# Moving the squares, the start of group 0 and two scalings in a fused attention and MLP kernel

## The chip, the cores and the metric

One core of one Trainium2 chip. The metric is device time in microseconds (us), the median of several executions; the six of the kernel before lie between 433.15 and 436.11 us. Each run also has a mean granted clock of TensorE over the span (1.0 is full speed); a stretch below it is called cold here, one at 1.0 warm. In the profiles PE is TensorE and PEld its weight loads, ACT is ScalarE, DVE is VectorE, Pool is GpSimd, and SPq is the queue on which SyncE issues transfers.

## The reference

For 8 batches and 12 heads, q and k (448 tokens of 64 numbers) are normed and weighted, softmax attention follows, and its output goes through a two-layer MLP:

```python
q_n, k_n = rmsnorm(q, g_q), rmsnorm(k, g_k)        # x / sqrt(mean(x*x) + 1e-6) * g
attn = softmax(q_n @ k_n.T / 8)
x = (attn @ v)  ->  (3584, 768)
h = x @ w_in                                        # 768 x 2048
g = max(h, 0) + alpha * min(h, 0)
out = g @ w_out                                     # 2048 x 768
```

## The kernel before

The 24 groups (`y`, three a batch, each of two pairs of heads) flow through all engines. For each group and each of q and k: a load into `nat`; squares on ACT or Pool; sums on DVE; two small ACT functions make the reciprocal root `rr`; a scaling to fp16 `qs` on DVE or Pool; transposes (on TensorE for the first six groups, by transposing transfers after that) into `qT` and `kT`. Then scores on TensorE, an exponential on ACT for each of seven tiles a group, sums over keys (`dn`), products with v (`av`), and the MLP (`hT` and `op`). Scores come in "bursts" of mostly two tiles. Where an instruction waited, those behind it on its engine waited too: the 2.93 us below are a case.

```python
def square(y, nm):
    src = nat[y, nm].rearrange("p h j d -> p (h j d)")
    sq = ld.tile([128, 2 * J, D], FP32, name="sq", tag="sq", bufs=4)
    sqf = sq.rearrange("p n d -> p (n d)")
    if y < 2:
        nc.scalar.activation(out=sqf, in_=src, func=AF.Square)
    else:
        nc.gpsimd.tensor_mul(out=sqf, in0=src, in1=src)
    sqs[y, nm] = sq

def scale(y, nm):
    t = ld.tile([128, J, 2, D], FP16, name="qs", tag="qs", bufs=4)
    eng = nc.vector if (y, nm) in ((0, "k"), (1, "q"), (2, "q"), (3, "q")) else nc.gpsimd
    eng.tensor_mul(out=t..., in0=nat[y, nm], in1=rr_t[y]...)     # cut
    qs[y, nm] = t

# where squares and sums are called: at = ahead of burst n, after = behind it      (cut)
    at(n - (6 if early else 4 if y <= 3 * G else 5), load_qk, y)
    for nm in "qk":
        (after if early else at)(n - 2, square, y, nm)
        if early:
            after(n, reduce, y, nm)
        else:
            jobs.setdefault(n, []).append((reduce, (y, nm)))
    roots[n + 1] = y

# the start                                                       (loads cut)
    spin(3)                     # filler matmuls
    spin(18, False)
    ...
    for nm in "qk":
        square(0, nm); reduce(0, nm)
    ...
    for nm in "qk":
        root(0, nm); scale(0, nm)
    ...
    square(1, "q"); turn(0); square(1, "k"); load_v(0); square(2, "q")
    for nm in "qk":
        reduce(1, nm)
    after(0, root, 1)
    for nm in "qk":
        after(0, scale, 1, nm)
    after(0, square, 2, "k")
    after(0, load_w_in, 0)
    ...
    roots[3] = 2                # root and both scalings of group 2 in burst 3
```

## Time and profile before

| | before |
|---|---|
| time, median | 433.94 us in the first 3 runs, 434.32 over 6 |
| span of the profiled run | 432.8 us |
| TensorE busy | 418.0 us, 97 % |
| ACT, DVE, Pool busy | 278.6, 204.3, 175.6 us |
| mean granted clock | 1.0 |
| chain that ended last | TensorE 81 %, ACT 5 %, DMA 5 %, DVE 4 %, Pool 2 % |

Busy shares over the whole span hide that the stages differ: one reads them by stretches of time. The lines for that are in the prediction. Bracketed at the end of a timeline line stands how long the engine was idle ahead of the instruction, and what ended that.

### The profile page before, as it was taken

Reading aid. Unit: us, or ns where it says so; the run is one execution under the profiler, and the core shown is the slowest. Engines: PE = TensorE matmul, PEld = TensorE weight load, DVE = VectorE, ACT = ScalarE, POOL = GpSimd, SP = SyncE. Lnnn points to the kernel's source line nnn. Section 1 sums busy time; section 2 is a strip of 40 time slices with the busy share of each in tenths; the row PEclk is TensorE's granted clock in tenths of the full one; section 3 lists DMA queues with packets and bytes.
Section 4 is the critical chain, followed back from the end, with each engine's and each line's share of the span. In section 5 each row is a group of like instructions: output and inputs, shape, how many; then the busy total and the mean of one; then the engine's idle time right before and its main releaser. Section 6 shows DMA issues by size and latency. Waiting matters only on the chain.

```text
span 432.8 us, 11487 instructions
## 1 busy us (share of the span) xinstructions
PE 418.0 (97%) x4965; PEld 216.8 (50%) x4965; DVE 204.3 (47%) x304; ACT 278.6 (64%) x385; POOL 175.6 (41%) x133
## 2 busy tenths in 40 slices
PE   8789899999999999999999999999999999999996
PEld 3344344444455445544555445554555445555554
DVE  3756564445545463546444463545453353233421
ACT  4898888668876677757667577757757577132300
POOL 5799693495464617083253626074133000000000
PEclk9999999999999999999999999999999999999999
DMA  8999899989787734967086743944082300211133
GB/s 192 236 235 215 146 211 190 206 151 200 171 120 179 180 82 67 201 109 186 20 157 142 164 118 63 202 99 113 20 153 52 77 1 21 56 38 31 25 73 75
DMA packets 70387, 53.85 MB, mean 124 GB/s; under 512 B 37424, under 2 KB 70336, under 8 KB 70336
## 3 DMA queue, kind: packets, MB, share of 16 engines
q1 hardware_dynamic: 55536, 40.19, 42.2%
q0 software_dynamic: 13984, 11.81, 18.1%
q10 hardware_dynamic: 816, 1.11, 1.0%
q8 instruction: 39, 0.64, 0.6%
q14 instruction: 12, 0.10, 0.1%
HBM read 45.62 MB, written 11.01 MB: 131 GB/s over the span
## 4 chain that ended last, share of the span: by engine, by line
PE 81%; ACT 5%; DMA 5%; DVE 4%; POOL 2%; issue 1%; DVEq 0%; POOLq 0%
PE op L365 26%; PE hT L327 20%; PE hTa L327 10%; PE sc L232 7%; PE opa L365 6%; PE dn L261 4%; PE av L261 4%; ACT expT L246 3%; DMA kT<-qs 3%; PE spin L394 2%; DMA nat<-in_k_dram 2%; PE avb L261 2%; DVE ss L154 2%; POOL qs L171 1%; DVE gT L355 1%
## 5 line engine op out<-in xcount | busy, mean ns | idle before, releaser
L246 ACT ACTIVATE expT<-sc,expb 128x896 f16<-128x896 f32 x168 | 161.4, 1003 | 36.5 <-PE sc L232 35.7
L365 PE MATMUL op<-w_out_sb,gT 128*128 128x384 f16 (+1 forms) x752 | 126.4, 323 | 0.0
L171 POOL TENSOR_TENSOR qs<-nat,rr 128x896 f16<-128x896 f32 x44 | 76.7, 1764 | 117.8 <-ACT rr L166 87.5
L365 PEld LDWEIGHTS <-gT 128*128 128x128 f16 x912 | 85.8, 98 | 65.4 <-issue 12.7
L327 PEld LDWEIGHTS <-w_in_sb 128*128 128x128 f16 x768 | 73.3, 98 | 75.1 <-issue 10.7
L327 PE MATMUL hT<-xT,w_in_sb 128*128 128x448 f16 x510 | 107.3, 353 | 1.9 <-DVE gT L355 1.1
L148 POOL TENSOR_TENSOR sq<-nat 128x896 f32<-128x896 f32 x44 | 73.4, 1681 | 40.5 <-DMA nat<-in_q_dram 36.6
L354 ACT ACTIVATE ah<-hT,cols 128x448 f16<-128x448 f32 x85 | 53.7, 633 | 44.2 <-PE hT L327 44.1
L355 DVE TENSOR_TENSOR gT<-hT,ah 128x448 f16<-128x448 f32 x85 | 52.8, 623 | 49.7 <-ACT ah L354 49.6
L377 DVE COPY osb<-op 128x384 f32<-128x384 f32 (+1 forms) x47 | 25.7, 548 | 86.8 <-PE op L365 86.8
L232 PE MATMUL sc<-qT,kT 64*32 64x448 f16 (+1 forms) x1092 | 53.6, 356 | 6.0 <-ACT expT L246 3.8
L154 DVE TENSOR_REDUCE ss<-sq 128x14 f32<-128x896 f32 x48 | 50.4, 1076 | 8.4 <-ACT sq L146 5.6
L327 PE MATMUL hTa<-xT,w_in_sb 128*128 128x448 f16 x246 | 53.2, 353 | 0.0
L354 ACT ACTIVATE ah<-hTa,cols 128x448 f16<-128x448 f32 x41 | 26.0, 633 | 31.4 <-PE hTa L327 31.4
L355 DVE TENSOR_TENSOR gT<-hTa,ah 128x448 f16<-128x448 f32 x41 | 25.5, 623 | 25.8 <-ACT ah L354 25.8
L232 PEld LDWEIGHTS <-kT 64*32 64x32 f16 (+1 forms) x1092 | 15.3, 93 | 38.6 <-issue 32.7
L365 PE MATMUL opa<-w_out_sb,gT 128*128 128x384 f16 x160 | 27.7, 327 | 0.6 <-DVE xT L312 0.6
L312 DVE TENSOR_TENSOR xT<-av,rden 128x896 f16<-128x896 f32 x16 | 17.4, 1090 | 17.6 <-PE av L261 14.2
L261 PEld LDWEIGHTS <-vt 64*32 64x32 f16 (+1 forms) x1260 | 18.9, 94 | 13.2 <-issue 2.2
L261 PE MATMUL dn<-expT,ones 64*32 64x448 f16 (+1 forms) x812 | 24.4, 350 | 1.1 <-issue 0.2
L261 PE MATMUL av<-expT,vt 64*32 64x448 f16 (+1 forms) x812 | 24.1, 350 | 0.0
L278 ACT ACTIVATE rden<-dn 128x896 f32<-128x896 f32 x16 | 14.5, 907 | 7.3 <-PE dn L261 7.3
(45 smaller groups left out, 162.0 us busy)
## 6 DMA issues: line engine op xcount, KB each, us to landing
out_dram<-osb SPq DMA_DIRECT2D x109, 96.0 KB, 2.3
nat<-in_q_dram SPq DMA_DIRECT2D x46, 224.0 KB, 5.3
nat<-in_k_dram SPq DMA_DIRECT2D x46, 224.0 KB, 5.5
vt<-in_v_dram POOLq DMA_DIRECT2D x16, 336.0 KB, 6.3
w_in_sb<-in_moe_w_in_dram POOLq DMA_DIRECT2D x12, 256.0 KB, 7.3
w_out_sb<-in_moe_w_out_dram POOLq DMA_DIRECT2D x4, 768.0 KB, 11.5
nat<-in_q_dram ACTq DMA_DIRECT2D x2, 224.0 KB, 4.5
nat<-in_k_dram ACTq DMA_DIRECT2D x2, 224.0 KB, 5.9
```

The lines of the kernel that those rows point to most:

```text
L148: nc.gpsimd.tensor_mul(out=sqf, in0=src, in1=src)
L154: nc.vector.tensor_reduce(out=ss_t[y][:, "qk".index(nm)].rearrange("p h j -> p (h j)").unsqueeze(2), in_=sqs[y, nm], axis=AXIS_X, op=ALU.add,)
L171: eng.tensor_mul(out=t.rearrange("p j h d -> p h j d"), in0=nat[y, nm], in1=rr_t[y][:, "qk".index(nm)].unsqueeze(3).broadcast_to((128, 2, ...
L232: nc.tensor.matmul(out=sc[ds(64 * g + m * c, m), par, :S].rearrange("p (j c) -> p j c", j=J), lhsT=kT[ds(64 * par, 64), j, g, ts(c, m)], r ...
L246: nc.scalar.activation(out=expT[y][:, j], in_=scs[y, j][:, :, :S], func=AF.Exp, scale=QK_SCALE, bias=expb[:, 0:1],)
L261: nc.tensor.matmul(out=accs[g][ds(m * h, m), :S], lhsT=weights(g, y, par, ts(c, m), j), rhs=expT[y][ds(64 * g, 64), j, par, :], start=(j = ...
L312: nc.vector.tensor_mul(out=x, in0=av[:, :, :S], in1=r)
L327: nc.tensor.matmul(out=hT[:, :S], lhsT=w_in_sb[:, g * G + i, ts(ft, 128)], rhs=xT[b][:, g, i, :], start=(i == 0 and g == 0), stop=(i == G ...
L354: nc.scalar.activation(out=ah, in_=hT[:, :S], func=AF.Copy, scale=alpha_sb[:, ft : ft + 1])
L355: nc.vector.tensor_max(out=gT[:, ft, ds((b & 1) * S, S)], in0=hT[:, :S], in1=ah)
L365: nc.tensor.matmul(out=ops[c][:, :PW], lhsT=gT[:, ft, ts(t, 128)], rhs=w_out_sb[:, ft, ds(oh * OH + c * PW, PW)], start=(ft == 0), stop=(f ...
L377: nc.vector.tensor_copy(out=o[:, ts(c, PW)], in_=ops[c][:, :PW])
```

## The change

It has three parts. The **start**: group 0 is squared and summed in pieces so that scores begin sooner; k of group 1 is squared on Pool; roots of groups 1 and 2 move inside a burst (`mid`), their scalings to the end of it. The **lead burst** (the one in which the first batch's attention ends and its MLP begins): two sums move behind the first MLP products. The **steady part**: from group 5 on, squares are called behind a burst, and so behind its scalings on Pool.

```diff
-        if y < 2:
+        if (y, nm) == (1, "q"):
             nc.scalar.activation(out=sqf, in_=src, func=AF.Square)
         else:
             nc.gpsimd.tensor_mul(out=sqf, in0=src, in1=src)
...
+    def part_square(nm, h, j, eng): ...       # and part_reduce, part_root, part_scale, part_turn, part_copy
...
         for nm in "qk":
-            (after if early else at)(n - 2, square, y, nm)
+            after(n - 2, square, y, nm)
...
-    spin(3)
-    spin(18, False)
+    spin(2)
+    spin(17, False)
...
+    for h in range(2):
+        part_square("q", slice(h, h + 1), full, nc.scalar)
+    for h in range(2):
+        part_reduce("q", slice(h, h + 1), full)
+    part_root("q", full)
+    part_scale("q", full, J, nc.gpsimd)
+    part_square("k", both, lo, nc.scalar)     # tokens 0 to 2 of 7
+    part_square("k", both, hi, nc.scalar)
...
-    after(0, root, 1)
-    for nm in "qk":
-        after(0, scale, 1, nm)
-    after(0, square, 2, "k")
-    after(0, load_w_in, 0)
+    mid[1] = 1
+    for nm in "qk":
+        after(1, scale, 1, nm)
+    after(1, square, 2, "k")
+    after(1, load_w_in, 0)
...
-    roots[3] = 2
+    mid[4] = 2
+    for nm in 'qk':
+        after(4, scale, 2, nm)
...
+            if n in mid and t == tiles[-1]:
+                root(mid[n])
             soft(*t)
...
-        if ups_first and n in dens:
+        if ups_first and n in dens and not lead:
...
-                if n in jobs:
+                if n in jobs and not (lead and done < 4):
...
         if not gaps[n] and n in turns:
+            if n < den_at[0]:
+                spin(1)
             turn(turns[n])
```

One consequence does not stand in the diff. Group 3's squares are called behind burst 4 too, by the loop that comes first; so in the built program they stand on Pool **ahead** of group 2's scaling of k.

More of the change, by code (lines that the diff above doesn't have):

```diff
@@ L169, in scale @@
         t = ld.tile([128, J, 2, D], FP16, name="qs", tag="qs", bufs=4)
-        eng = nc.vector if (y, nm) in ((0, "k"), (1, "q"), (2, "q"), (3, "q")) else nc.gpsimd
+        eng = nc.vector if nm == "q" and 0 < y <= G else nc.gpsimd
         eng.tensor_mul(
@@ L176, in scale, with part_square, part_reduce @@
         qs[y, nm] = t
+    tops = {}
+    def part_square(nm, h, j, eng):
+        if ("sq", nm) not in tops:
+            tops["sq", nm] = ld.tile([128, 2 * J, D], FP32, name="sq", tag="sq", bufs=4)
+        o = tops["sq", nm].rearrange("p (h j) d -> p h j d", h=2)[:, h, j]
+        src = nat[0, nm][:, h, j]
+        if eng is nc.scalar:
+            nc.scalar.activation(out=o, in_=src, func=AF.Square)
+        else:
+            eng.tensor_mul(out=o, in0=src, in1=src)
+    def part_reduce(nm, h, j):
+        if 0 not in ss_t:
+            ss_t[0] = ld.tile([128, 2, 2, J], FP32, name="ss", tag="ss", bufs=4)
+        nc.vector.tensor_reduce(
+            out=ss_t[0][:, "qk".index(nm), h, j].unsqueeze(3),
+            in_=tops["sq", nm].rearrange("p (h j) d -> p h j d", h=2)[:, h, j],
+            axis=AXIS_X, op=ALU.add,
+        )
@@ new lines, in part_root, with part_scale @@
+    def part_root(nm, j):
+        if 0 not in rr_t:
+            rr_t[0] = ld.tile([128, 2, 2, J], FP32, name="rr", tag="rr", bufs=4)
+        n = "qk".index(nm)
+        rr, ss = rr_t[0][:, n, :, j], ss_t[0][:, n, :, j]
+        nc.scalar.activation(out=rr, in_=ss, func=AF.Ln, scale=1.0 / D, bias=epsb[:, 0:1])
+        nc.scalar.activation(out=rr, in_=rr, func=AF.Exp, scale=-0.5)
+    def part_scale(nm, j, n, eng):
+        if (0, nm) not in qs:
+            qs[0, nm] = ld.tile([128, J, 2, D], FP16, name="qs", tag="qs", bufs=4)
+        eng.tensor_mul(
+            out=qs[0, nm][:, j].rearrange("p j h d -> p h j d"),
+            in0=nat[0, nm][:, :, j],
+            in1=rr_t[0][:, "qk".index(nm), :, j].unsqueeze(3).broadcast_to((128, 2, n, D)),
+        )
@@ new lines, in part_turn, with part_copy @@
+    def part_turn(nm, js):
+        if ("ps", nm) not in tops:
+            t = psf.tile([128, 512], FP32, name="tps", tag="mm")
+            tops["ps", nm] = t[:, :S].bitcast(FP16).rearrange("p (j c) -> p j c", j=J)
+        for j in js:
+            nc.tensor.transpose(
+                tops["ps", nm][:, j, :], qs[0, nm][:, j].rearrange("p h d -> p (h d)"), ident
+            )
+    def part_copy(nm, j, eng):
+        if (0, nm) not in qkT:
+            qkT[0, nm] = att.tile([128, J, 2, 64], FP16, name=f"{nm}T", tag=f"{nm}T", bufs=4)
+        o = qkT[0, nm].rearrange("p j g c -> p j (g c)")[:, j]
+        tp = tops["ps", nm][:, j]
+        if nm == "k":
+            nc.vector.tensor_scalar(
+                out=o, in0=tp, scalar1=gain[:, 0:1], scalar2=None, op0=ALU.mult
+            )
+        elif eng is nc.scalar:
+            nc.scalar.copy(out=o, in_=tp)
+        else:
+            eng.tensor_copy(out=o, in_=tp)
@@ L211, in turn @@
             o = t.rearrange("p j g c -> p j (g c)")
-            if nm == "q" and y == 0:
-                nc.scalar.copy(out=o, in_=tp)
-            elif nm == "q":
+            if nm == "q":
                 nc.vector.tensor_copy(out=o, in_=tp)
@@ L443 @@
     NB = len(bursts)
-    prep, post, roots = {}, {}, {}
+    prep, post, roots, mid = {}, {}, {}, {}
     def at(n, f, *a):
@@ L573 @@
     load_qk(2)
-    spin(3)
-    spin(18, False)
+    spin(2)
+    spin(17, False)
     ct = psf.tile([128, 512], FP32, name="ct", tag="mm")
     nc.tensor.transpose(ct[:, : NF + 2], rows, ident32[: NF + 2, : NF + 2])
-    spin(1)
-    for nm in "qk":
-        square(0, nm)
-        reduce(0, nm)
+    K0 = 3
+    both, full, lo, hi = slice(0, 2), slice(0, J), slice(0, K0), slice(K0, J)
+    for h in range(2):
[6 more added lines that the diff above has]
+    part_square("k", both, hi, nc.scalar)
+    part_reduce("k", both, lo)
+    part_reduce("k", both, hi)
+    part_root("k", lo)
+    part_scale("k", lo, K0, nc.vector)
+    part_root("k", hi)
+    square(1, "q")
     nc.vector.tensor_copy(out=cols, in_=ct[:, : NF + 2])
-    for nm in "qk":
-        root(0, nm)
-        scale(0, nm)
     nc.vector.tensor_mul(
@@ L589 @@
     )
-    square(1, "q")
-    turn(0)
+    part_turn("q", range(J))
+    part_turn("k", range(K0))
+    part_copy("q", full, nc.vector)
+    part_copy("k", lo, nc.vector)
+    load_v(0)
     square(1, "k")
-    load_v(0)
+    part_scale("k", hi, J - K0, nc.vector)
+    reduce(1, "q")
     square(2, "q")
+    after(0, part_turn, "k", range(K0, J))
+    after(0, part_copy, "k", hi, nc.vector)
+    after(0, reduce, 1, "k")
+    mid[1] = 1
     for nm in "qk":
-        reduce(1, nm)
-    after(0, root, 1)
-    for nm in "qk":
-        after(0, scale, 1, nm)
-    after(0, square, 2, "k")
-    after(0, load_w_in, 0)
+        after(1, scale, 1, nm)
+    after(1, square, 2, "k")
+    after(1, load_w_in, 0)
     for nm in "qk":
```

## The prediction

> **What bounds the kernel now.** I read four views: the page, the table by stretches of time, the waits of the matrix engine, and the timeline of the first 45 us. First the table by stretches (PE, PEld, DVE, ACT, POOL: busy us and instructions; then clock, DMA share, GB/s):
>
> ```profile
> 12.85:35.00 22.15, 19.02 (x305) 8.71 (x306) 14.97 (x18) 21.41 (x29) 20.69 (x15) 1.00 1.18 232
> 35.00:55.00 20.00, 17.96 (x163) 8.40 (x164) 11.38 (x17) 15.95 (x25) 16.15 (x15) 1.00 0.98 178
> 55.00:110.00 55.00, 52.28 (x545) 25.70 (x544) 28.38 (x42) 42.18 (x59) 35.13 (x25) 1.00 1.10 192
> 110.00:165.00 55.00, 54.85 (x671) 27.69 (x670) 27.55 (x41) 40.63 (x59) 24.81 (x16) 1.00 0.64 137
> ```
>
> From 110 us on TensorE is full (54.85 of 55.00 us), so nothing done to Pool, DVE or ACT there moves the end. From 12.85 to 35 us the full engines are ACT (21.41 of 22.15) and Pool (20.69); TensorE's 19.02 contain filler ("spin", 1.02 us each). So 12.85 to 35 us is bound by the stream of softmax exponentials on ACT and by Pool, which prepares q and k for it. A microsecond lost or won there moves everything behind it, since TensorE has no slack later to absorb it.
>
> The waits of TensorE over the whole span:
>
> ```profile
> PE sc L232 <- ACT expT L246: 3.8, 8, 1.0
> PE sc L232 <- DVE kT L217: 1.2, 2, 0.8
> PE hT L327 <- DVE gT L355: 1.1, 3, 0.5
> PE sc L232 <- DVE kT L192: 0.7, 2, 0.5
> ```
>
> Only "kT L192" (0.7 us) belongs to the steady part's q/k preparation: that is what any reordering of Pool after 56 us can win.
>
> The timeline (start, us, engine, line, instruction) where the change works:
>
> ```profile
> 8.68 1.69 POOL L171 TENSOR_TENSOR qs<-nat,rr 128x896 f16<-128x896 f32 x1 [4.37 <-ACT rr L166]
> ...
> 12.39 0.95 ACT L146 ACTIVATE sq<-nat 128x896 f32<-128x896 f32 x1
> ...
> 12.85 0.57 PE L232 MATMUL sc<-qT,kT 64*64 64x448 f16 x8 [0.78 <-DVE kT L217]
> ...
> 13.29 1.90 ACT L246 ACTIVATE expT<-sc,expb 128x896 f16<-128x896 f32 x2
> ...
> 15.69 1.09 DVE L171 TENSOR_TENSOR qs<-nat,rr 128x896 f16<-128x896 f32 x1 [0.90 <-ACT rr L166]
> 15.73 2.60 POOL L171 TENSOR_TENSOR qs<-nat,rr 128x896 f16<-128x896 f32 x1 [0.87 <-ACT rr L166]
> ...
> 19.91 1.48 POOL L124 DMA_DIRECT2D w_in_sb<-in_moe_w_in_dram  x2
> 21.38 0.73 POOL L127 DMA_DIRECT2D w_in_sb<-in_moe_w_in_dram  x1
> ...
> 22.36 2.58 POOL L171 TENSOR_TENSOR qs<-nat,rr 128x896 f16<-128x896 f32 x1 [0.24 <-ACT rr L166]
> 24.90 3.31 POOL L148 TENSOR_TENSOR sq<-nat 128x896 f32<-128x896 f32 x2
> ```
>
> The first exponential starts at 13.29 us. Pool scales group 2's k at 22.36, as soon as its root is there, and squares group 3 behind it. The same scaling takes 1.69 us alone and 2.6 us beside a DVE scaling.
>
> [...] 2.60 and 2.58 us for Pool's scaling beside DVE's 1.09, 1.69 beside a reduction. [...] an ACT root on 128x14 takes 0.21 us, a square on 128x896 0.95; my line is 0.2 us + 0.84 ns an element.
>
> **The change, part by part** (instruction orders of both built programs compared).
>
> 1. *Start of group 0.* q's square goes by heads, k's chain in token parts of 3 and 4; the copy of qT goes from ACT to DVE, and 1,k's square from ACT to Pool. Estimated pieces: square of 448 elements 0.57, 384: 0.52, 512: 0.63; reductions (1.08 for 896) 0.61, 0.54, 0.68; DVE scaling of the first k part 0.54. From q's landing at 5.31: squares end 6.40, second reduction 7.1, root 7.66; Pool scales q 7.75 to 9.44 (was 8.68 to 10.37). k landed at 7.20, but its squares now stand behind q's root: 7.63 to 8.73, reductions to 9.44, first part scaled 9.98. Then on DVE in order the copy of cols (0.18), gain (0.15), qT (0.62), first kT part (0.36): 11.27. Scores at about 11.3 instead of 12.85, first exponential about 11.8: **1.5 us earlier**.
>
> 2. *Group 1.* Its root now follows three exponentials instead of two, and waits for the second reduction, which on DVE stands behind k's second scaling, the first reduction (1.08), kT's second part (0.45): about 14.8, root ready 15.4 (was 15.65). Pool's scaling of k, 2.6 us beside DVE's, ends 18.1 (was 18.33). The transposes of group 1 thus come hardly earlier, and ACT, one tile ahead, idles for them. Of the 1.5 us some 0.2 are left.
>
> 3. *Group 2: the step that decides.* Before, Pool went: scaling of 1,k; square of 2,k; w_in issues; scaling of 2,k; two squares of group 3. The built program of the change has the two squares of group 3 **ahead** of the scaling of 2,k (it is called behind burst 4, after squares that stand there already). From 18.1: square 1.65, w_in issues 1.48 + 0.73, so 22.0; two squares 3.31, so 25.3; up to 0.9 for the collision with DVE's scaling of 2,q (2.6 less 1.69), so 26.2; scaling 1.69, so **27.8 instead of 24.94: 2.9 us later**. [...] the transposes of 2,k stand ahead of the scores of tile 12, so ACT runs dry although tiles of group 1 are left. Its exponential comes at 28.8 instead of 25.9.
>
> 4. *Lead burst.* Both reductions of group 5 (2.07 us at 41.67) move from ahead of the first gT products to between later ones. gT waits then only for ah (about 43.0 instead of 43.66): **0.5 us won**, the wait of hT on gT at 44.32.
>
> 5. *Steady part.* Squares go behind the scalings of a burst on Pool, same instructions. q and k reach their transposing DMAs some 3.3 us (two squares) earlier; worth at most the 0.7 us of kT L192: I take **0.6**.
>
> Sum: +2.9 − 0.5 − 0.6 = +1.8; a little less for what group 1's lead leaves (0.2): +1.6, so 435.5 us.
>
> **Rivals.** *A: the gain of the start survives*, because Pool reaches the squares of group 3 early enough to hide them. For it: Pool idles in the trace at 11.7 to 13.2. Against: until 22.0 Pool is laid out solidly, and the root of group 2 stands at 22.3. Then step 3 is gone, and 1.1 (one exponential and a bit) + 0.5 + 0.6 are won: about 431.7. *B: [...]* If 1,k's square starts on Pool before DVE's second k scaling (about 11.0 against 11.3), DVE waits 1.4 us, the root of group 1 slips by 1.2 and all of step 3 with it: about 436.7. Conversely, if DVE's scaling of 2,q is what waits, Pool saves 0.9: 434.6. *C: transfers bound the start.* DMA share is 0.87 before 12.85 us; the landing of 2,q (13.18) might slip with v's issue 0.9 us earlier. Then the square of 2,q, ending at 15.2, delays Pool by a few tenths. *D: the idle of TensorE cools it.* [...] step 3 leaves about 2.5. The trace has only 1.00 in the table above, so I give it little: up to +1.5 us.
>
> **Range and chances.** Step 3 may cost 2.0 to 4.0, steps 4 and 5 bring 0.3 to 1.5: 434.5 to 437.5. Rival A, to which I give one in six, pulls the lower end to 431.8; B and D together the upper to 438.2. Two per cent are 8.7 us, far more than any of these: faster 0.02, same 0.96, slower 0.02.
>
> **What would show it.** The first expT at about 11.8 (step 1); group 1's transposes within 0.4 us of 17.8 to 18.9 (step 2); Pool's second-group scaling ending about 27.8, behind two squares, and a gap of some 3 us in ACT's exponentials ahead of it (step 3); the first gT in the lead burst at once behind its ah (step 4); no wait for kT L192's successor (step 5), with TensorE as full from 110 us as before. The prediction is wrong if Pool's squares of group 3 end before group 2's root, or if the delay of 2.9 us is made up before 45 us by waits that I took for fixed.

## The result, and the profile after

The changed kernel took **438.56 us** (median of 6; 437.58 to 440.02), the kernel before 434.32. The ratio is 1.0097, with a 95 % interval of 1.0068 to 1.0126. A ratio here is the mean time of one kernel's fast runs over that of the other's in the same rounds, so not quite the ratio of the medians. The direction was foreseen; the size (+1.6 us over the first 433.94, range to 438.2) was not: the kernel lost about 4.2 us. The profiled run is the slowest of the six and one of the two coldest (440.02 us, clock 0.987), so what its profile shows of the clock is more than in a usual run (438.2 us, 0.996).

The same table by stretches, of the changed kernel (PE, PEld, DVE, ACT, POOL busy; then clock, DMA share, GB/s):

```profile
12.85:35.00 22.15, 16.65 (x162) 6.88 (x160) 14.45 (x13) 15.26 (x22) 15.52 (x14) 0.85 1.14 222
35.00:55.00 20.00, 18.85 (x282) 9.37 (x275) 12.90 (x17) 17.49 (x26) 16.98 (x14) 1.00 0.85 150
55.00:110.00 55.00, 51.70 (x540) 25.38 (x538) 28.08 (x41) 40.91 (x58) 39.01 (x28) 0.97 1.15 201
110.00:165.00 55.00, 54.85 (x607) 27.29 (x605) 27.91 (x44) 40.73 (x57) 21.32 (x14) 1.00 0.66 144
```

In the stretch that bounds the start, ACT works 15.26 us instead of 21.41; 4.77 us of the difference are one gap in the stream of exponentials, shown below. And the clock is 0.85. From 110 us on TensorE is as full as before (54.85 us). Three of TensorE's longest waits:

```profile
PE tps L268 <- DVE qs L171: 2.9, 1, 2.9
...
PE sc L292 <- DVE kT L254: 1.2, 1, 1.2
PE hT L387 <- DVE gT L415: 1.0, 1, 1.0
```

The first is new: group 2's transposes wait 2.9 us for a scaling on DVE, not on Pool. The timeline shows why. First the place in the kernel before, where the 13th exponential is the fifth of the eight at 22.17, so at about 25.9 us:

```profile
22.17 7.45 ACT L246 ACTIVATE expT<-sc,expb 128x896 f16<-128x896 f32 x8
...
22.30 1.09 DVE L171 TENSOR_TENSOR qs<-nat,rr 128x896 f16<-128x896 f32 x1 [0.64 <-ACT rr L166]
```

Then the changed kernel, where the 13th is the one at 29.75:

```profile
11.62 2.80 ACT L306 ACTIVATE expT<-sc,expb 128x896 f16<-128x896 f32 x3 [0.81 <-PE sc L292]
...
18.71 1.91 ACT L306 ACTIVATE expT<-sc,expb 128x896 f16<-128x896 f32 x2 [0.97 <-PE sc L292]
...
21.50 3.35 POOL L148 TENSOR_TENSOR sq<-nat 128x896 f32<-128x896 f32 x2
...
22.32 5.12 DVE L171 TENSOR_TENSOR qs<-nat,rr 128x896 f16<-128x896 f32 x1 [1.27 <-ACT rr L166]
...
24.79 1.71 POOL L171 TENSOR_TENSOR qs<-nat,rr 128x896 f16<-128x896 f32 x1
...
27.51 1.68 PE L268 MATMUL tps<-ident,qs 128*128 128x128 f16 x14 [2.93 <-DVE qs L171]
...
29.75 1.90 ACT L306 ACTIVATE expT<-sc,expb 128x896 f16<-128x896 f32 x2 [4.77 <-PE sc L292]
...
30.00 1.86 PE L454 MATMUL spin<-gT 128*128 128x448 f32 x2
```

Pool began two squares at 21.50 and went from them straight into the scaling of k. DVE's scaling of q, ready at 22.32, is recorded at 5.12 us, where it takes 1.09 elsewhere: it ended at 27.44, 0.94 us behind the last of Pool's three instructions (26.50). TensorE then had idled for 2.93 us, and the filler at 30.00 takes 1.86 us instead of the 1.02 of other places: the granted clock was 0.50 from 27.00 to 33.82 us. The packed traces have a record of the clock, from about 7 us on. In all 14 profiles a cold spell is at half clock and lasts 3.41 us or 6.83, save at the very end; here one of 6.83 begins at 27.00 us, 2.43 us into those 2.93 of idleness, and one of 3.41 at 85.02, after 1.24 and 0.62 us of idleness with four matmuls between (the 16 matmuls there took 4.44 us instead of 2.77), while the kernel before has none but at its end. A spell of 3.41 us takes 0.004 off the mean clock of a run (estimate: half of 3.41 over 438), so that 0.996, 0.992 and 0.988 go with one, two and three of them.

### The profile page after: what moved, and what is told of

Same layout as the page of the kernel before. It is cut to its first block, busy times and chain, and to the rows that moved or that the text cites.

```text
span 437.9 us, 11496 instructions
## 1 busy us (share of the span) xinstructions
PE 420.8 (96%) x4964; PEld 217.8 (50%) x4964; DVE 207.9 (47%) x309; ACT 278.0 (63%) x387; POOL 176.1 (40%) x134
## 4 chain that ended last, share of the span: by engine, by line
PE 80%; DMA 3%; DVE 2%; POOL 0%; issue 0%; ACT 0%
PE op L425 27%; PE hT L387 20%; PE hTa L387 10%; PE opa L425 7%; PE sc L292 6%; PE dn L321 4%; PE av L321 4%; DMA kT<-qs 3%; PE avb L321 2%; DVE osb L437 1%; DVE ss L154 0%; POOL sq L148 0%; DVE xT L372 0%; DVE gT L415 0%; PE tps L268 0%
## 5 line engine op out<-in xcount | busy, mean ns | idle before, releaser
L171 POOL TENSOR_TENSOR qs<-nat,rr 128x896 f16<-128x896 f32 x43 | 74.2, 1746 | 151.8 <-issue 101.3
L148 POOL TENSOR_TENSOR sq<-nat 128x896 f32<-128x896 f32 x45 | 74.6, 1680 | 7.7 <-DMA nat<-in_q_dram 5.0
L154 DVE TENSOR_REDUCE ss<-sq 128x14 f32<-128x896 f32 x46 | 48.4, 1076 | 0.8 <-POOL sq L148 0.7
L425 PE MATMUL opa<-w_out_sb,gT 128*128 128x384 f16 x160 | 29.4, 340 | 0.6 <-DVE xT L372 0.6
```

What stands on the lines that cost most here:

```text
L154: nc.vector.tensor_reduce(out=ss_t[y][:, "qk".index(nm)].rearrange("p h j -> p (h j)").unsqueeze(2), in_=sqs[y, nm], axis=AXIS_X, op=ALU.add,)
L171: eng.tensor_mul(out=t.rearrange("p j h d -> p h j d"), in0=nat[y, nm], in1=rr_t[y][:, "qk".index(nm)].unsqueeze(3).broadcast_to((128, 2, ...
L425: nc.tensor.matmul(out=ops[c][:, :PW], lhsT=gT[:, ft, ts(t, 128)], rhs=w_out_sb[:, ft, ds(oh * OH + c * PW, PW)], start=(ft == 0), stop=(f ...
```

## The experiments

The runs came in three sets, each on one chip and with its own runs of the kernel before (medians 434.6, 434.93 and 435.27 us). Every ratio below is to those; the 1.0097 above is to the runs of its own measurement. **Theory:** Pool's order ahead of group 2's scalings, with the wait of DVE for Pool that it brings (5.12 us instead of 1.09), costs most of the loss, and the idle that it leaves (2.93 us) cools TensorE. **Rivals:** the split start costs the time; the reordered steady part does; DVE's wait or the clock has no part in it.

### Set 1

**Only Pool's order** (`e1_scale_first`). The changed kernel with group 2 scaled right behind its root; the built program differs on Pool alone, in one swap.

```diff
                 root(mid[n])
+                if mid[n] == 2:
+                    for nm in "qk":
+                        scale(2, nm)
...
-    for nm in 'qk':
-        after(4, scale, 2, nm)
```

> The changed kernel with one swap on Pool: the scaling of group 2's k stands ahead of the two squares of group 3 instead of behind them; nothing else differs on any engine. Theory [...]: DVE's scaling of 2,q lasts about 1.1 us instead of 5.12, Pool's of 2,k about 2.6, the granted clock from 12.85 to 35 us is 1.00, the exponentials from the 13th on come 4.5 us earlier, and the time is about 433 us, 0 to 2 us under the kernel before. Rival (the new start or the reordered steady part cost the time): stays at 437 to 438.5 us.

Measured: 435.29 us, ratio 1.0028 (1.0004 to 1.0053). Its timeline at the place:

```profile
22.40 1.09 DVE L171 TENSOR_TENSOR qs<-nat,rr 128x896 f16<-128x896 f32 x1 [1.27 <-ACT rr L166]
22.45 2.58 POOL L171 TENSOR_TENSOR qs<-nat,rr 128x896 f16<-128x896 f32 x1 [0.87 <-ACT rr L166]
...
26.02 3.70 ACT L306 ACTIVATE expT<-sc,expb 128x896 f16<-128x896 f32 x4 [0.96 <-PE sc L292]
```

DVE takes 1.09 us, and the 13th exponential comes at 26.02 instead of 29.75. One swap removes 0.69 of the 0.97 %, 3.0 us (0.58 %, if it is held against the repeat of set 3). The expected time was missed by 2 us all the same: 26.02 is where the kernel before stood (25.9), so that the start's lead is gone by then even in the right order, and the remaining 0.28 % arise later. A part of them is one cold run (438.69 us at 0.987): by the medians 0.16 % are left.

**Pool writes only** (`e2_pool_no_read`). Group 3's squares on Pool become fills of the same tile, which read nothing: the question is whether DVE's scaling still takes 5.12 us. Its output is wrong, which doesn't matter for the time.

```diff
+        elif y == 3:
+            nc.gpsimd.memset(sqf, 1.0)
         else:
             nc.gpsimd.tensor_mul(out=sqf, in0=src, in1=src)
```

> The changed kernel with the two squares of group 3 on Pool replaced by fills of the same tile (wrong result on purpose for that group): Pool's order stays, but the two instructions only write SBUF. [...] DVE's scaling of 2,q ends by 24.5 us or soon after instead of 27.44 and lasts 1.1 to 2.8 us. Rival (Pool's order alone delays group 2[...]): DVE's scaling still lasts over 4 us. The fill may be shorter than the square, so the time itself is no clean measure; about 434 to 436 us expected.

Measured: 434.37 us, ratio 0.9999 (0.998 to 1.0019).

```profile
21.57 1.67 POOL L148 MEMSET sq<- 128x896 f32 x2
...
22.42 1.09 DVE L173 TENSOR_TENSOR qs<-nat,rr 128x896 f16<-128x896 f32 x1 [1.27 <-ACT rr L168]
23.17 1.89 POOL L173 TENSOR_TENSOR qs<-nat,rr 128x896 f16<-128x896 f32 x1
```

DVE starts in the middle of Pool's fills and isn't held up (1.09 us); Pool's scaling, which reads, takes 1.89 us instead of 1.69, beside the last third of a microsecond of DVE's. So what DVE waited for in the changed kernel were Pool instructions that read. The time is no measure of that, since two fills are also 1.7 us shorter than two squares.

**The gap filled** (`e3_fill_gap`). Four fillers instead of one ahead of group 2's transposes.

```diff
-                spin(1)
+                spin(4 if turns[n] == 2 else 1)
```

> The changed kernel with four filler matmuls instead of one ahead of group 2's transposes (3 us more of filler in the gap of 2.93 us in which TensorE idles). Theory that the cold clock is a part of the cost: the clock from 12.85 to 35 us is 1.00, the transposes come at about the same 27.6 us, the scores and denominators behind them take their usual times, and 1 to 1.5 us of the 4.2 come back: about 437.2 us. Rival (the clock does not matter there, since ACT is the bound): within 0.3 us of the changed kernel's 438.5.

Measured: 437.92 us, ratio 1.0086 (1.0053 to 1.0118): not to be told from the changed kernel's 1.0097. The profiled run was warm behind the gap: from the 13th exponential to the root of group 3 it took 29.14 to 32.71, 3.57 us, as in the run with the swap (26.02 to 29.59), where the changed kernel took 4.48 (29.75 to 34.23). But it was cold at the start (0.97 in the first 12.85 us, 0.88 from there to 24). Its DVE scaling took 3.48 us, so it had waited for two of Pool's instructions, not for three as in the changed kernel's profile. The expected 1.3 us therefore aren't shown in the time, and warmth alone did not bring them: the run of the six with a clock of 1.0 took 438.36 us.

**The steady part alone** (`e4_steady_only`), on the kernel before.

```diff
-            (after if early else at)(n - 2, square, y, nm)
+            after(n - 2, square, y, nm)
```

> The kernel before with one part of the change alone: from group 5 on the squares go behind a burst's scalings on Pool. The prediction said 0.6 us won. The theory now, from the changed kernel's trace (the transposing transfer of k issued at 69.55 landed only after 13.2 us among the weight loads): transfers bound the wait for k, nothing is won, and 0 to 1 us may be lost: 434 to 435 us.

Measured: 434.71 us, ratio 1.0009 (0.9992 to 1.0027): neutral. The queue of SyncE in this run shows the transposing transfers of group 6, and DVE's row the operation that waits for the second:

```profile
63.87 1.34 SPq L181 DMA_TRANSPOSE qT<-qs  x1
65.51 4.00 SPq L181 DMA_TRANSPOSE kT<-qs  x1
...
78.90 0.45 DVE L192 TENSOR_SCALAR kT<-kT,gain 128x896 f16<-128x896 f16 x1 [4.00 <-DMA kT<-qs]
```

The same in the kernel before:

```profile
68.92 3.37 SPq L181 DMA_TRANSPOSE kT<-qs  x1
...
77.32 0.45 DVE L192 TENSOR_SCALAR kT<-kT,gain 128x896 f16<-128x896 f16 x1 [2.81 <-DMA kT<-qs]
```

k's transfer was issued at 65.51, 3.4 us earlier than before (68.92), as predicted. But DVE, which waits for it, went on at 78.90 instead of 77.32: 13.4 us from issue, where it had been 8.4. Pool issued weight loads just before (60.33 in this run, 60.47 before), and DVE went on only after these were through: in the packed traces the last packet of Pool's transfers ends at 78.16 us here and at 75.74 before. No run moved the loads, so that they bound the tile is read from the traces, not tested. The scores' wait for kT grew from 0.2 to 1.39 us.

### Set 2

**The lead burst alone** (`e5_lead_only`), on the kernel before.

```diff
-        if ups_first and n in dens:
+        if ups_first and n in dens and not lead:
...
-                if n in jobs:
+                if n in jobs and not (lead and done < 4):
```

> The kernel before with one part of the change alone: in the lead burst the two reductions of group 5 move from ahead of the first gT products to between later ones. The prediction said 0.5 us won; the trace of the run with the swapped scaling shows the 12 matmuls of hT behind it at 46.71 instead of 47.26 us. Theory: that half microsecond stays to the end, 433.5 to 434.2 us, or at most 0.6 us under the kernel before. Rival: a later wait of hT on gT or on kT takes it back, and the time is that of before within 0.2 us.

Measured: **434.02 us against 434.93**, ratio 0.9981 (0.9967 to 0.9995). It is the one part that helps by itself, and this kernel beats both. Its six runs all had the clock 1.0. The waits of hT on gT, 1.1 us in three in the kernel before, are 0.6 us in two:

```profile
PE hT L327 <- DVE gT L355: 0.6, 2, 0.4
```

**The start in the right order, nothing else** (`e7_start_fixed`): the swap of the first run, with lead burst and steady part put back.

> The new start alone (groups 0 to 2 as in the changed kernel, group 2's scaling ahead of group 3's squares), steady part and lead burst as before. Theory (the first exponential is 1.6 us earlier, but the scaling of groups 1 and 2 on Pool takes all of it back): the exponential after group 2's transposes at 26.0 us as before (25.9), time within 0.5 us of the kernel before. Rival (the start is worth a microsecond and the steady part hides it): 433 us or less.

Measured: 435.31 us, ratio 1.0009 (0.9992 to 1.0026): a first exponential 1.6 us earlier brings nothing. The profiled run was also cold at the start (clock 0.96 and 0.95 in the first two stretches), with the 13th exponential at 26.99.

**The same with the lead burst** (`e8_fixed_lead`).

> The changed kernel with group 2's scaling ahead of group 3's squares and with the steady part as before, so new start and lead burst without the reordered squares. Theory (the steady part costs about 0.4 us and, through the longer wait for kT near 80 us, sometimes a cold clock): about 433.6 us, 1.0 to 1.7 us under the run with the swapped scaling and the steady part (435.29); no wait of the scores for kT over 0.7 us. Rival (the steady part is neutral): 435 us.

Measured: 434.81 us, ratio 0.9997 (0.9981 to 1.0014); the profiled run, warm throughout, 434.14. The run with the swap and the steady part had 1.0028: behind the new start, the steady part costs 0.3 %. That is less than expected (1.0 to 1.7 us): the medians are 0.5 us apart, or 0.8 if each is held against its own kernel before. The one cold run told of above counts in the 0.3 %, and the interval of the difference nearly reaches zero.

**Both k scalings on DVE** (`e9_dve_scale`), and no filler ahead of the transposes of groups 1 and 2; the rest as in the run before. Beside DVE's, Pool's scaling of 2,k had taken 2.58 us; two on DVE in a row would take 2.2 (estimate: twice 1.09).

```diff
-        eng = nc.vector if nm == "q" and 0 < y <= G else nc.gpsimd
+        eng = nc.vector if nm == "q" and 0 < y <= G or y in (1, 2) else nc.gpsimd
...
-            if n < den_at[0]:
-                spin(1)
             turn(turns[n])
```

> As the run before it in this set (new start, lead burst, steady part as before), and also: k of groups 1 and 2 is scaled on DVE behind q instead of on Pool, and there is no filler ahead of their transposes. Theory [...]: transposes of group 2 end about 0.6 to 1 us earlier than 25.65 us, and the time is 0.5 to 1.2 us under the run before it, about 432.7 us. Rival (ACT or the later waits take it back): no difference.

Measured: 435.78 us, ratio 1.0029 (1.0004 to 1.0054): a miss.

```profile
15.19 3.58 DVE L171 TENSOR_TENSOR qs<-nat,rr 128x896 f16<-128x896 f32 x2 [0.64 <-ACT rr L166]
...
23.90 2.09 DVE L171 TENSOR_TENSOR qs<-nat,rr 128x896 f16<-128x896 f32 x2 [1.81 <-ACT rr L166]
```

Group 2's pair took 2.09 us, as expected; group 1's took 3.58, with Pool squaring 2,k meanwhile (2.18 us from 15.64). TensorE waited 1.8 us for it and was at a clock of 0.92 from 12.85 to 35 us. Yet this profiled run is the fastest of the six (433.81 us, under the kernel before), so it can't show what made the others slow (434.54 to 437.81).

### Set 3

**The changed kernel again** (`e12_after_again`), unaltered.

> The changed kernel once more, unaltered, for comparison on the same chip. Expected 438 to 439 us, 0.9 to 1.0 % over the kernel before; DVE's scaling of 2,q between 3.5 and 5.2 us[...]; TensorE cold for some microseconds behind it.

Measured: 438.98 us, ratio 1.0086 (1.0052 to 1.012). This time DVE waited for two of Pool's instructions, not for three:

```profile
23.60 3.48 DVE L171 TENSOR_TENSOR qs<-nat,rr 128x896 f16<-128x896 f32 x1 [1.27 <-ACT rr L166]
...
26.06 2.56 POOL L171 TENSOR_TENSOR qs<-nat,rr 128x896 f16<-128x896 f32 x1
```

DVE came in between Pool's squares and its scaling, so Pool's k scaling was the late one, ending at 28.62. In these six runs a colder one was also a slower one:

| granted clock, mean of the run | time, us |
|---|---|
| 0.999 | 437.04 |
| 0.996 | 438.55, 438.30 |
| 0.992 | 439.41 |
| 0.988, 0.987 | 440.72, 439.97 |

The warmest run is still 1.8 us above that set's kernel before (435.27). The six runs of the first measurement fit: 437.58 to 438.89 at 0.995 and 0.996, 440.02 and 439.38 at 0.987 and 0.988. This is no law: the fill of the gap has 438.36 us at 1.0, and the next run below 438.49 at 0.987 but 440.89 at 0.992.

**Pool as long, but not reading** (`e10_pool_same_time`): each square of group 3 becomes two fills, so that Pool's times stay. Its output is wrong, which doesn't matter for the time.

```diff
+        elif y == 3:
+            for _ in range(2):
+                nc.gpsimd.memset(sqf, 1.0)
```

> The changed kernel with each of the two squares of group 3 on Pool replaced by two fills of the same tile (wrong result on purpose): four fills of 0.84 us take the 3.35 us of the two squares, so Pool's order and its times stay, and only its reading of SBUF is gone. Theory [...]: DVE's scaling of 2,q lasts 1.1 us from 22.4, Pool's of 2,k still ends at about 26.5, so that only k's transposes wait; group 2's first exponential at about 27.4 instead of 29.75, TensorE idles under 2 us and mostly stays warm; 436 to 437 us, 2 us under the changed kernel. Rival (Pool's order is the whole cost): within 0.7 us of the changed kernel.

Measured: 438.16 us, ratio 1.0073 (1.0039 to 1.0108). The place itself went as the theory has it:

```profile
21.53 3.48 POOL L149 MEMSET sq<- 128x896 f32 x4
...
22.38 1.09 DVE L174 TENSOR_TENSOR qs<-nat,rr 128x896 f16<-128x896 f32 x1 [1.27 <-ACT rr L169]
...
24.98 1.68 POOL L174 TENSOR_TENSOR qs<-nat,rr 128x896 f16<-128x896 f32 x1
...
27.65 3.70 ACT L309 ACTIVATE expT<-sc,expb 128x896 f16<-128x896 f32 x4 [2.61 <-PE sc L295]
```

DVE takes 1.09 us, the exponential comes at 27.65 instead of 29.75, TensorE stays warm to 35 us (clock 1.00). But in the time only 0.13 % less than the changed kernel of the same set are seen, within the noise: the rival's number. In the profiled run, the slowest of its six, the gain was given back at 38 us, where TensorE stood 2.0 us before a matmul of hT for "issue" (0.25 us in the kernel before) and was cold behind it (0.91 from 35 to 55 us):

```profile
39.98 0.55 PE L390 MATMUL hT<-xT,w_in_sb 128*128 128x448 f16 x2 [2.01 <-issue]
```

So the part of DVE's wait by itself is shown at the place, not in the end time. The fills that were 1.8 us shorter left no loss (0.9999), these leave 0.73 %; so without DVE's wait, too, what carries the loss is how long Pool is kept from its scaling.

What TensorE stood for in those 2.0 us is not shown; the packed traces have one thing that went with it. In ten of the profiles two of these matmuls, which else start 0.19 us apart, start 0.35 to 2.36 us apart, and in each TensorE goes on 1.3 to 1.7 us after a 16 KB packet of the kind "instruction" (queue 8) has landed: at 39.98 after 38.59 us here, at 36.30 after 34.76 in the kernel before. In the last run below, with three fillers more ahead, the pause comes three matmuls earlier. No run tested whether the one hangs on the other.

**The start alone as built** (`e6_start_only`): the changed kernel with lead burst and steady part put back.

> The changed kernel with lead burst and steady part as before, so its start alone, with group 2's scaling still behind group 3's squares. Theory by sums (start as built 3.0 for the order on Pool and 0.4 for the rest, steady part 0.4 to 1.3, lead burst -0.8 to -0.5): 437.5 to 438.3 us. Rival (the parts do not add): 436 or less, or over 439.

Measured: 438.22 us, ratio 1.0065 (1.004 to 1.0091). The start with the wrong order carries most of the loss by itself; DVE's scaling took 5.12 us again.

**A try for more** (`e11_group1_dve`): 1,k scaled on DVE, the first w_in issues ahead of the square of 2,k, three more fillers at the start; Pool's order right, the lead burst new and the steady part as before.

```diff
-        eng = nc.vector if nm == "q" and 0 < y <= G else nc.gpsimd
+        eng = nc.vector if nm == "q" and 0 < y <= G or y == 1 else nc.gpsimd
...
-    after(1, square, 2, "k")
     after(1, load_w_in, 0)
+    after(1, square, 2, "k")
...
-    spin(17, False)
+    spin(20, False)
```

> A try for a kernel better than both: new start with group 2's scaling ahead of the squares, lead burst, steady part as before; k of group 1 scaled on DVE behind q, with the first w_in issues ahead of the square of 2,k so that Pool reads nothing meanwhile; three more fillers at the start to keep TensorE warm. Theory: the two DVE scalings of group 1 take 2.2 us undisturbed (3.58 in the earlier try), group 1's transposes end about 0.5 us earlier, clock 1.00 in all stretches: 433.5 us, 0.5 under the lead burst alone (434.02). Rival (a later wait takes it back): 434 to 435.

Measured: 438.97 us, ratio 1.0081 (1.0044 to 1.0118): a clear miss. Pool was through with its issues at 17.53, just before DVE's second scaling, and began the square (2.29 us from there): the two scalings took 4.23 us. The clock was 0.81 from 12.85 to 24 us and 0.79 from there to 35, in spite of the fillers. Its two runs at 1.0 took 436.24 and 437.08 us, still over the kernel before.

### What the runs add up to

| kernel | start | Pool's order right | lead burst | steady part | ratio to before |
|---|---|---|---|---|---|
| `e4_steady_only` | | | | x | 1.0009 |
| `e5_lead_only` | | | x | | 0.9981 |
| `e7_start_fixed` | x | x | | | 1.0009 |
| `e8_fixed_lead` | x | x | x | | 0.9997 |
| `e1_scale_first` | x | x | x | x | 1.0028 |
| `e6_start_only` | x | no | | | 1.0065 |
| changed kernel | x | no | x | x | 1.0097, again 1.0086 |

The order on Pool is worth 0.56 % without the other parts (1.0065 less 1.0009) and 0.69 % with them (1.0097 less 1.0028): 2.4 to 3.0 us of some 4. The rest is the steady part behind the new start (0.31 %, where it is 0.09 % alone), less the lead burst. Each of these differences is uncertain by 0.3 to 0.4 % (estimate, from the intervals of the two runs in it): the order's part is clear of that, the steady part's hardly.

## Why the prediction was wrong

- **Step 1 held.** The first exponential came at 11.62 us (11.8 predicted).
- **Step 2 held in kind.** Group 1's transposes began at 17.17 instead of 17.81, so 0.6 us of the lead were left there and not 0.2, and ACT idled 0.97 us for them. The runs go further: even in the right order nothing is left of the start's lead at the 13th exponential (26.02 against 25.9).
- **Step 3 is the term that was mis-sized.** Order and place were right, and the gap in the exponentials is there. The prediction took 2.9 us, with the *Pool* scaling of 2,k last at 27.8. In the profiled run that ended at 26.50; the DVE scaling of 2,q ended at 27.44, so that all 14 transposes, not 7, stood behind it. The exponential came at 29.75, not at 28.8. The sentence that failed is in rival B: "if DVE's scaling of 2,q is what waits, Pool saves 0.9: 434.6". It took a wait of DVE for harmless, because it held DVE up for one Pool instruction at most. DVE waited for three in a row (5.12 us), or for two (3.48). How much of this reached the end time is not settled: without DVE's wait (`e10_pool_same_time`) the 13th exponential came at 27.65, earlier than the 28.8 predicted, and the kernel still lost 0.73 %. So a second assumption failed too: that a microsecond lost at the start moves everything behind it by as much.
- **Rival D, kept small, came true in the profile.** "I give it little: up to +1.5 us." The clock was 0.85 from 12.85 to 35 us. From the 13th exponential to the root of group 3 the changed kernel took 4.48 us, where warm runs take 3.57. So at that root it was 4.6 us behind the run with the swap (34.23 against 29.59): 3.03 by the transposes' later begin (27.51 against 24.48), 0.70 from there to the exponential, and 0.91 after it. The last two fall in the cold spell from 27.00 us on.
- **Step 4 held.** The lead burst alone brings 0.19 % (0.8 us).
- **Step 5 failed.** It left out the weight loads that Pool issues ahead of k's transfer: from its issue to DVE's going on it was 13.4 us, where it had been 8.4 (that the loads made the difference was not tested). The prediction took 0.6 us won. The scalings were 3.4 us earlier, as it said, but DVE could go on with k's transposed tile only 1.6 us later, and the part is neutral alone. Behind the new start it costs more. In the run with the swap the wait for kT was 1.82 us, and the 16 matmuls behind it took 4.44 us instead of 2.77, cold; with the steady part alone it was 1.39 us and they stayed warm (2.76 us). That this is why the parts do not add is argued from these profiles and not shown by a run of its own.

Errors of the same sign make up the 3 us between 435.5 and 438.56: in the profiled run, colder than most, 0.95 us in step 3 (29.75 against 28.8) and 0.91 by the clock behind it; and 1.0 to 1.9 us in step 5, where 0.6 won were 0.09 to 0.31 % lost. This is a rough account, since the parts do not simply add. Open stay: how much of the end time is due to DVE's wait alone or to the clock alone, and why the start of some runs is cold. The new start has one wide filler fewer at the beginning and another one fewer ahead of group 0's transposes, but three narrow ones more did not cure it.

## What to carry to other kernels

When a change moves an instruction on one engine, ask what now stands ahead of it in the built order, and what on another engine waits for that: here DVE's scaling waited for two or three reading Pool instructions in a row (3.48 and 5.12 us instead of 1.09), not only for the one that ran. In the end time only the order is shown to count. A pipeline that starts earlier only to wait at the next group gained nothing here (the start in the right order: 1.0009), and a new gap on TensorE (2.93 us) went with a cold spell (6.83 us at half clock). Measure the parts of a bundle one by one: here the smallest part, two conditions in the lead burst, was the only one to keep.
